# Attention weights, v, x and W_in as pairs of fp16 words, and two heads' value products on the two column halves of TensorE

## Chip, cores and metric

The kernel runs on one core of one Trainium2 chip. The metric is the device time of one execution in microseconds, as the median of several runs; lower is better. Engines are named as the profile names them: PE is TensorE (PEld its weight loads), DVE VectorE, ACT ScalarE, POOL GpSimd, SP the engine that issues the DMAs.

## What is computed

Decayed causal attention for 8 batches of 8 heads (576 positions, 64 columns a head), and on its result, laid out as 4608 tokens of 512 columns, a feed-forward layer with a softmax-weighted activation and a layer norm:

```python
def _attn_ref(q, k, v, f):
    scores = np.matmul(q, k.transpose(0, 1, 3, 2)) / np.sqrt(D)
    cum = np.cumsum(np.log(np.clip(f, 0.0001, 1.0)), axis=-1)
    scores = np.where(causal, -1e9, scores + cum[..., :, None] - cum[..., None, :])
    attn = np.exp(scores - scores.max(-1, keepdims=True))
    attn = attn / (attn.sum(-1, keepdims=True) + 1e-09)
    return np.matmul(attn, v)

def _moe_ref(x, w_in, w_out, g_ln):        # x: (4608, 512), d_ff 1024
    h = x @ w_in
    solu = h * softmax(h)
    ln = (solu - solu.mean(-1)) / np.sqrt(solu.var(-1) + 1e-06) * g_ln
    return ln @ w_out
```

The weights arrive as float64 and are unpacked to fp32 by integer operations on the chip.

## The kernel before

Products keep fp32 accuracy by splitting an operand into a high and a low word: `hi` is the value rounded to the matmul's type and `lo` the rest. Attention and the product with W_in use fp32r words (one pass of the array, operands of four bytes); the product with W_out already uses fp16 words.

**Attention** runs over 32 pairs of heads (`NPAIR` = 4 pairs in each of 8 batches), and in each pair over five tiles of queries: one of 64 rows, then four of 128. Tiles 0 to 2 are half 0 of a pair (320 queries), tiles 3 and 4 half 1 (256 queries). `load` brings q, k and v; `parts` and `split_qk` split q and k; `split_v` has POOL write v's high word (L558) and low word (L560) into `vs`, and two DMAs lay a zero-padded first block into `v0`. `scores` (L590, L591) writes score tiles to PSUM; DVE adds the mask and takes the minimum (L595), ACT takes the exponential (L598), POOL divides by the row sum (L611) into the weights P. `transposes` turns P through TensorE (L637), ACT copies the high word out of PSUM (L320) and DVE the low one (L645). `values` (L677) multiplies v and P for one head: for every block `j` of keys (three in half 0, five in half 1) one matmul with P's high word against v's high and low words side by side (128 columns of weights, so that the two results land on the two halves of PSUM's partitions), and one with P's low word against v's high word (64 columns). ACT copies one half of the partitions to `xt` (L698) and DVE adds the other (L699). The half 0 of the first four pairs, called native or early, runs in plain fp32 while the weights are still being unpacked.

**The layer** runs over 36 blocks of 128 tokens. ACT and POOL split a block of `xt` into `xh` (L710) and `xl` (L711); 24 matmuls of 512 columns (L715 to L717) give h in `hps`; DVE, ACT and POOL make the activation; 24 fp16 matmuls (L781 to L783) multiply with W_out; ACT scales the result (L813) and a DMA stores it.

**Order.** Every operation goes to a `Plan` with its engine, an assumed duration, its dependencies and a due time from tables at the top (`DUE`, `EARLY`, `AT_P`, `AT_L`, ...). The planner puts them in order for each engine; nothing is reordered on the chip, so that table numbers change the order of the whole program. Where its plan leaves PE idle in the first 140 us or after 690 us, it puts in matmuls of the identity into an unused PSUM region that nothing reads (L870, called fills below):

```python
for _ in range(int(share(t) * (y - x) / (256 * COLUMN))):
    nc.tensor.matmul(dst[:, :256], blank[:, :P], blank, start=True, stop=True)
```

Of the kernel before, what the change touches and what calls it, by code (L numbers as in the profile page):

```python
# [8 lines left out]
F32 = mybir.dt.float32  # L9
# [9 lines left out]
P = 128  # L19
# [18 lines left out]
PE, ACT, DVE, POOL, SP = range(5)  # L38
COLUMN, TRANSPOSE, SHORT = 0.4525, 109.0, 0.4215
# [3 lines left out]
W_UP, W_TOP = (1, 1, 1, 1, 3, 3, 1, 1), (1, 2, 1, 1, 1, 1, 2, 1)  # L43
# [139 lines left out]
DUE = dict(load=-21.603, split=-26.826, upper=-18.618, v=-13.364, S=((-15.632, -9.737), (-9.429, -3.796), (-5.211, -1.211), (-3.144, -0.221), (-0.983, 2.057)), T=((-5.374,), (-58.596,), (0.469, -2.051), (11.613, 15.096), (12.825, -17.362, 18.063)), V=((16.261, 10.309), (23.822, 24.94)))  # L183
EARLY = dict(load=-59.299, split=-31.676, upper=-77.592, v=4.813, S=((69.953, -64.026), (12.978, -19.27), (-10.825, -113.484), (16.361, 2.865), (6.007, 30.266)), T=((56.285,), (-26.169,), (4.567, -42.406), (18.877, 18.035), (-89.589, -1.353, 13.794)), V=((0.943, -17.263), (43.016, -5.748)))
PAIR = 23.152
C_OUT = 49.124
START = 86.674
HALF = ((21.727, 4.145), (48.927, -3.824))
W_IN = (-31.427, 49.165)
W_OUT = (167.026, 57.23)  # L190
LOAD = (91.563, -22.285)
W_SCALE = 216.178
W_DMA = (-107.022, -70.722)
LAYER = PAIR * NPAIR / 4.5
AT_P = (-22.203, 4.549, -13.13, 1.257, -1.491, 0.321, 0.679, -1.806, 5.637, 4.27, 2.052, -51.442, 0.817, -4.873, -1.256, -59.967, 1.404, 7.193, 6.528, -0.523, 0.88, -85.501, -15.204, -17.336, -23.387, -16.669, -16.683, -14.175, -4.607, -35.105, -17.856, -8.142)
AT_L = (7.435, 11.184, -2.371, 1.053, -11.997, -5.199, -4.486, -8.251, -8.484, -1.657, -2.698, 2.39, 4.153, -41.008, -6.573, -1.246, 1.043, 4.319, 5.403, -1.43, -3.146, -3.847, -8.617, -4.13, 2.145, 1.851, -3.014, -7.085, -1.035, 1.207, -5.225, -2.466, 0.361, 3.687, 6.959, 0.375)
FIRST = 96.162

STAGES = (1.419, 1.059, 4.523, 23.041, 11.635)
# [3 lines left out]
def tile_kernel(ctx: ExitStack, tc: tile.TileContext, qk, v, f, w_in, w_out, g_ln, out):  # L203
# [39 lines left out]
    v0 = [[sb(f"v0_{n}_{h}", 2 * D, dtype=F32R) for h in range(2)] for n in range(2)]  # L243
# [143 lines left out]
    dma(-90, g_sb, g_ln, 4, writes=[("g",)])  # L387

    def weights(src, n, due, t, tk, w, wk, first=(), clear=()):
# [9 lines left out]
        dma(due + W_DMA[n // NCC] if n else -98, t, src.bitcast(I32).rearrange("p (c n) -> p c n", n=512), 712 if tk[0][0] != "xt" else 940, reads=first, writes=tk)  # L401
# [23 lines left out]
    def prepare_w_in(c, due):  # L425
        w, wk = w_buffer(c % 3)
        weights(w_in[c], c, due, lambda: buf(f"wo_{c}", "raw", 4, DM, dtype=I32), [("raww", c)],
                w, wk, summed if c else ())
        copied(WI_H[c], {ACT: 1050, DVE: 690, POOL: 1130}, due, wi_h[:, c, :], w, [wk], [("wi", c)])
        op(WI_L[c], 2360 if WI_L[c] == POOL else 1170, due, lambda: (nc.gpsimd if WI_L[c] == POOL else nc.vector).tensor_tensor(  # L430
            wi_l[:, c, :], w, wi_h[:, c, :].bitcast(F32), ALU.subtract), reads=[wk, ("wi", c)], writes=[("wil", c)], port=True)
# [7 lines left out]
    def prepare_w_out(c, due):  # L439
        if c % 2:  # L440
            t, tk = xt[:, :, S:S + 512].bitcast(I32), [("xt", 1, x, hp) for x in range(2) for hp in range(NPAIR)]
# [7 lines left out]
        op(DVE, 1200, due, lambda: nc.vector.tensor_reduce(  # L449
            top[:, 2 * c:2 * c + 2], w().rearrange("p (r n) -> p r n", r=2), axis=AX.X, op=ALU.max, apply_absolute_value=True), [wk], [("top", c)])  # L450

    def scale_w_out(due):
        key = ("t", "scale")

        def across():
            nc.vector.tensor_tensor(top[:, :NFC], top[:, :NFC], g_sb, ALU.mult)
            nc.vector.tensor_reduce(top[:, NFC:], top[:, :NFC], axis=AX.X, op=ALU.max, apply_absolute_value=True)
        op(DVE, 320, due, across, [("g",), *(("top", c) for c in range(NFC // 2))], [("top",)])
        op(PE, 150, due, lambda: nc.tensor.transpose(ps_t[plan.place[key]][:1, 0, :], top[:, NFC:], ident), [("top",), ("const",)], [key], take=key, dense=False)
# [8 lines left out]
        op(PE, 150, due, lambda: nc.tensor.matmul(ps_t[plan.place[key]][:, 1, :2], ones, scales[:1, :], start=True, stop=True), [("scales",), ("ones",)], [key], dense=False)

        def factors():  # L470
            nc.vector.tensor_scalar(scales[:, 0:1], ps_t[plan.place[key]][:, 1, 0:1], 2.0 ** -24, None, ALU.mult)
            nc.vector.tensor_scalar(scales[:, 1:2], ps_t[plan.place[key]][:, 1, 1:2], 2.0 ** 13, None, ALU.mult)
            nc.vector.tensor_scalar(sg, g_sb, scales[:, 1:2], None, ALU.mult)
        op(DVE, 500, due, factors, [key, ("g",)], [("scales",), ("sg",)])
# [33 lines left out]
    def load(p, at):  # L508
# [140 lines left out]
    def values(p, half, h, at):  # L649
# [10 lines left out]
        def product(j):  # L660
# [3 lines left out]
            if j == 0 and native:  # L664
                rows, slot = row(h), 0
# [248 lines left out]
```

## Time and profile before

| | us |
|---|---|
| median of three runs | 785.98 (783.48 to 786.21) |
| the profiled execution | 783.74 |
| its span, first to last instruction | 782.0 |
| PE busy | 768.1 (98%) |
| DVE busy | 595.1 (76%) |
| ACT busy | 515.0 (66%) |
| POOL busy | 499.2 (64%) |

TensorE's granted clock was 0.999 of its full 2.4 GHz over the span. A matmul's record lasts from its start until its result has left the array, so that records of successive matmuls overlap; what a matmul takes of PE's time is read from start to start, not from the record's length.

### The profile page before, as it was taken

Reading aid. Unit: us, or ns where it says so; the run is one execution under the profiler, and the core shown is the slowest. Engines: PE = TensorE matmul, PEld = TensorE weight load, DVE = VectorE, ACT = ScalarE, POOL = GpSimd, SP = SyncE. Lnnn points to the kernel's source line nnn. Section 1 sums busy time; section 2 is a strip of 40 time slices with the busy share of each in tenths; the row PEclk is TensorE's granted clock in tenths of the full one; section 3 lists DMA queues with packets and bytes.
Section 4 is the critical chain, followed back from the end, with each engine's and each line's share of the span. In section 5 each row is a group of like instructions: output and inputs, shape, how many; then the busy total and the mean of one; then the engine's idle time right before and its main releaser. Section 6 shows DMA issues by size and latency. Waiting matters only on the chain.

```text
span 782.0 us, 15882 instructions
## 1 busy us (share of the span) xinstructions
PE 768.1 (98%) x4817; PEld 589.8 (75%) x4817; DVE 595.1 (76%) x1865; ACT 515.0 (66%) x1317; POOL 499.2 (64%) x688
## 2 busy tenths in 40 slices
PE   8999999999999999999999999999999999999998
PEld 6767678887787778777788877777777778776665
DVE  7789979997688768777679888787788688774333
ACT  5556668886677667765678777676677577664433
POOL 4556559776578577766757787777776686542230
PEclk9999999999999999999999999999999999999999
DMA  8656677766467666866658757867776656120000
GB/s 272 205 186 185 176 190 203 196 180 183 128 136 198 161 166 166 171 153 178 157 142 190 167 141 188 182 142 176 182 191 169 164 138 171 49 61 14 28 28 27
DMA packets 117012, 120.06 MB, mean 154 GB/s; under 512 B 64000, under 2 KB 78592, under 8 KB 116160
## 3 DMA queue, kind: packets, MB, share of 16 engines
q1 hardware_dynamic: 116928, 119.06, 60.3%
q8 instruction: 38, 0.62, 0.3%
q14 instruction: 46, 0.38, 0.2%
HBM read 39.11 MB, written 10.03 MB: 63 GB/s over the span
## 4 chain that ended last, share of the span: by engine, by line
PE 78%; DMA 8%; DVE 5%; SPq 3%; POOL 3%; issue 2%; ACT 1%; POOLq 0%; DVEq 0%; ACTq 0%
PE ps_o L677 12%; PE ps_t L637 10%; PE ps_o L781 7%; PE hps L715 7%; PE hps L716 7%; PE hps L717 7%; PE ps_o L782 7%; PE ps_o L783 7%; PE ps L590 5%; PE ps L591 5%; SPq L326 3%; DMA zz<-z 2%; DMA wo_raw<-in_w_in_dram 1%; DVE p L595 1%; PE ps_t L765 1%
## 5 line engine op out<-in xcount | busy, mean ns | idle before, releaser
L611 POOL TENSOR_SCALAR p<-p,ri 128x448 f32<-128x448 f32 (+4 forms) x320 | 183.1, 588 | 92.3 <-DVE ri L607 72.6
L598 ACT ACTIVATE p<-p,nm 128x192 f32<-128x192 f32 (+4 forms) x320 | 177.8, 557 | 63.7 <-DVE nm L595 54.1
L645 DVE TENSOR_TENSOR ptl_f32r<-ps_t,pth_f32r 128x384 fp32r<-128x384 f32 (+3 forms) x272 | 135.9, 518 | 26.9 <-ACT pth_f32r L320 24.5
L595 DVE CUSTOM_DVE_ANT_0 p<-ps,mask 128x192 f32<-128x192 f32 (+4 forms) x320 | 130.5, 422 | 30.7 <-PE ps L591 22.6
L320 ACT ACTIVATE pth_f32r<-ps_t 128x384 fp32r<-128x384 f32 (+3 forms) x272 | 119.3, 462 | 49.4 <-PE ps_t L637 46.7
L637 PE MATMUL ps_t<-ident,p 128*128 128x128 f32 x800 | 124.6, 274 | 1.4 <-POOL p L611 0.7
L715 PE MATMUL hps<-wi_h,xh 128*128 128x512 f32 x288 | 121.8, 423 | 0.4 <-DVE e L733 0.4
L590 PE MATMUL ps<-ks_f32r,qs_f32r 128*64 128x64 f32 (+4 forms) x360 | 120.0, 344 | 1.0 <-DVE nm L595 0.5
L637 PEld LDWEIGHTS ps_t<-ident,p 128*128 128x128 f32 x800 | 95.8, 140 | 25.3 <-DVE ptl_f32r L645 3.0
L716 PE MATMUL hps<-wi_l,xh 128*128 128x512 f32 x288 | 113.7, 395 | 0.0
L717 PE MATMUL hps<-wi_h,xl 128*128 128x512 f32 x288 | 113.7, 395 | 0.0
L781 PE MATMUL ps_o<-wo_f,zz 128*128 128x512 f16 x280 | 107.4, 384 | 1.9 <-DMA zz<-z 1.8
L782 PE MATMUL ps_o<-wo_f,zz 128*128 128x512 f16 x280 | 106.1, 379 | 1.1 <-DVE wo_f L479 1.1
L783 PE MATMUL ps_o<-wo_f,zz 128*128 128x512 f16 x280 | 106.1, 379 | 0.0
L591 PE MATMUL ps<-kz_f32r,qz 128*64 128x64 f32 (+4 forms) x360 | 103.5, 295 | 0.0
L677 PE MATMUL ps_o<-pth_f32r,vs_f32r 128*128 128x128 f32 (+1 forms) x368 | 95.1, 272 | 0.0
L590 PEld LDWEIGHTS ps<-ks_f32r,qs_f32r 128*128 128x128 f32 (+1 forms) x360 | 65.0, 181 | 16.9 <-DVE nm L595 7.8
L677 PE MATMUL ps_o<-ptl_f32r,vs_f32r 128*64 128x128 f32 (+1 forms) x368 | 71.8, 262 | 0.0
L711 POOL TENSOR_TENSOR xl<-xt,xh 128x512 fp32r<-128x512 f32 x36 | 46.0, 1278 | 40.2 <-ACT xh L710 39.7
L677 PEld LDWEIGHTS ps_o<-pth_f32r,vs_f32r 128*128 128x128 f32 x368 | 68.8, 189 | 2.5
L591 PEld LDWEIGHTS ps<-kz_f32r,qz 128*128 128x128 f32 (+1 forms) x360 | 65.2, 181 | 4.5
L726 DVE TENSOR_REDUCE st<-hps 128x1 f32<-128x1024 f32 x36 | 43.9, 1220 | 31.4 <-PE hps L717 30.9
(147 smaller groups left out, 1490.9 us busy)
## 6 DMA issues: line engine op xcount, KB each, us to landing
raw<-in_qk_dram SPq DMA_DIRECT2D x64, 288.0 KB
ks_f32r<-hi SPq DMA_DIRECT2D x128, 144.0 KB
raw<-in_v_dram SPq DMA_DIRECT2D x32, 288.0 KB
kz_f32r<-raw SPq DMA_DIRECT2D x64, 144.0 KB
out_dram<-y SPq DMA_DIRECT2D x35, 256.0 KB
qs_f32r<-hi SPq DMA_DIRECT2D x56, 144.0 KB
qs_f32r<-raw SPq DMA_DIRECT2D x56, 144.0 KB
qz<-hi SPq DMA_DIRECT2D x56, 80.0 KB
```

Source lines behind the costliest of these rows:

```text
L590: nc.tensor.matmul(dst, qs(p)[:, h, q0:q0 + nq], ks(p)[:, h, cols], start=True, stop=False)
L591: nc.tensor.matmul(dst, z[:, h, z0:z0 + nq], kz(p)[:, h, cols], start=False, stop=True)
L598: op(ACT, E_NS[i], at + 1.3, lambda: nc.scalar.activation(pr, pr, AF.Exp, bias=x, scale=-1.0, accum_out=sm[m][i][:nq, h, 0:1]), [("nm", m, ...
L611: op(POOL, N_NS[i], at + 2.8, lambda g=g, pg=pg: nc.gpsimd.tensor_scalar(pg, pg, r_[:, g:g + 1], 1.0, ALU.mult, ALU.mult), [("ri", m, i)], ...
L637: nc.tensor.transpose(tp[:, s, :], pt[i][:, k * P:(k + 1) * P], ident)
L677: nc.tensor.matmul(o[:mm, a:w], vv, mv, start=(j == 0 and x == 0), stop=(j == order[-1] and x == 0))
L715: nc.tensor.matmul(hps[:, sl], xh[:, c, :], wi_h[:, c, sl], start=(c == 0), stop=False)
L716: nc.tensor.matmul(hps[:, sl], xh[:, c, :], wi_l[:, c, sl], start=False, stop=False)
L717: nc.tensor.matmul(hps[:, sl], xl[:, c, :], wi_h[:, c, sl], start=False, stop=(c == NCC - 1))
L781: nc.tensor.matmul(o, zz[a][:, 0, j], wo(0, k), start=(k == 0), stop=False)
L782: nc.tensor.matmul(o, zz[a][:, 0, j], wo(1, k), start=False, stop=False)
L783: nc.tensor.matmul(o, zz[a][:, 1, j], wo(0, k), start=False, stop=(k == NFC - 1))
```

## The change

- P, v, x and W_in become two fp16 words. P is multiplied by 2^14 in the division by the row sum (`P_UP`). v and W_in are multiplied by a power of two found on the chip: `scale_w_in` takes the maximum of all four blocks of W_in before any is split; `scale_v` takes sums of squares of v on ACT, once for the early blocks, once for the rest of batch 0 and once for each later batch. Each of the eleven scales (`scale`, W_out's among them, which had its own code before) is a chain of DVE, PE (a transpose), DVE, PE (a product with ones), DVE. The layer undoes the scales in the operations after h (`unscale`), with one small DVE operation more per block.
- `values` takes both heads of a pair into one PSUM region. Block 0 of keys, which holds 64 rows of each head, is three full-width matmuls (L719) against a block-diagonal v. Every other block is six matmuls with 64 columns of weights (L723): high by high, low by high and high by low, each for head 0 into PSUM partitions 0 to 63 and for head 1 into 64 to 127.
- x leaves PSUM as two fp16 words (ACT, then DVE) straight into `x16`, so that the layer's split (L710, L711) is gone.
- v is loaded in a batch's four pairs together (`load_v`), its high word is made by POOL and its low word by DVE; the copies into `v0` are gone.
- The maxima for W_out's scale move from DVE (L449) to ACT (squares). All tables of due times are new.

```diff
+P_UP, SMALL = 2.0 ** 14, 2.0 ** -20
+VN, VN_EARLY = 2 * NQ, 6
...
-    wi_h, wi_l = (sb(f"wi_{x}", NCC, DFF, dtype=F32R) for x in "hl")
+    wi_h, wi_l = (sb(f"wi_{x}", NCC, DFF, dtype=F16) for x in "hl")
...
+    def scale_v(r, due):
...
+            op(ACT, 320 + 55 * (e - a), due[1] + 0.1 * hp, lambda hp=hp: nc.scalar.activation(
+                junk[:, :e - a], vraw[b % 2][:, hp, a:e], AF.Square, scale=SMALL, accum_out=tops[y][:, c + hp:c + hp + 1]),
...
     def split_v(p, at):
-        op(POOL, 650, at, lambda: nc.gpsimd.tensor_scalar(vs(p)[:, :, 0, :], rv, 1.0, 1.0, ALU.mult, ALU.mult),
-        op(POOL, 1395, at, lambda: nc.gpsimd.tensor_tensor(vs(p)[:, :, 1, :], rv, vs(p)[:, :, 0, :].bitcast(F32), ALU.subtract),
...
+        op(POOL, 860, at, lambda: nc.gpsimd.tensor_scalar(v16[m][:, 0], vraw[b % 2][:, hp], sv, 1.0, ALU.mult, ALU.mult), rk, [("v16", m)])
+        op(DVE, 740, at, lambda: nc.vector.scalar_tensor_tensor(v16[m][:, 1], vraw[b % 2][:, hp], sv, v16[m][:, 0], ALU.mult, ALU.subtract),
...
-    def values(p, half, h, at):
+    def values(p, half, at):
...
-            for x in (0, 1) if j != order[-1] else (1, 0):
...
-                    vv = (vs(p)[:, slot].rearrange("p a d -> p (a d)") if j else v0[m][h])[:, :mm]
-                    mv = ptx(p, half, x)[:, c0 + a:c0 + w]
-                nc.tensor.matmul(o[:mm, a:w], vv, mv, start=(j == 0 and x == 0), stop=(j == order[-1] and x == 0))
...
+            for n, (x, y) in enumerate(((0, 0), (1, 0), (0, 1))):
+                if j == 0:
+                    nc.tensor.matmul(o[:, :w], v16[m][:, x, :2].rearrange("p t d -> p (t d)"), ptx(p, half, y)[:, :w], start=(n == 0), stop=False)
+                    continue
+                for h in range(2):
+                    c0 = 256 * (2 * j - 1 + h)
+                    nc.tensor.matmul(o[row(h), a:w], v16[m][:, x, 2 * j + h], ptx(p, half, y)[:, c0 + a:c0 + w], start=False, stop=(end and n == 2))
...
-            nc.tensor.matmul(hps[:, sl], xh[:, c, :], wi_h[:, c, sl], start=(c == 0), stop=False)
+            x_h, x_l = (t[:, c, c0:c0 + P] for t in x16)
+            nc.tensor.matmul(hps[:, sl], x_h, wi_h[:, c, sl], start=(c == 0), stop=False)
```

**The order on PE, one pair's half 0 in the middle of the program.** Before, head 0 alone (`v0` and `vs` are v, `pth` and `ptl` P's high and low words, `ps_o` the PSUM region; the last number is the moving operand's columns):

```order
L677 MATMUL ps_o0_127<-pth_0_f32r_1547,v0_0_0_65 128x320
L677 MATMUL ps_o0_127<-ptl_0_f32r_1552,v0_0_0_65 64x320
L677 MATMUL ps_o0_127<-pth_0_f32r_1547,vs_0_f32r_809 128x128
L677 MATMUL ps_o0_127<-ptl_0_f32r_1552,vs_0_f32r_809 64x128
L677 MATMUL ps_o0_127<-ptl_0_f32r_1552,vs_0_f32r_809 64x256
L677 MATMUL ps_o0_127<-pth_0_f32r_1547,vs_0_f32r_809 128x256
```

And now, the end of the full-width products and the beginning of those on halves (`v16` is v; a weight load stands by itself for fp16):

```order
L719 LDWEIGHTS v16_0_80
L719 MATMUL ps_o0_158<-ptl_0_f16_1807,v16_0_80 128x320
L685 MATMUL ps_t0_156<-ident_61,p_0_65 128x128
L723 LDWEIGHTS v16_0_80
L723 MATMUL ps_o0_158<-pth_0_f16_1795,v16_0_80 64x128
```

The six rows of one head became three full-width matmuls and twelve on halves for both heads, the halves alternating; there are 180 of L719 in the program (84 of 320 columns, 96 of 256) and 1104 of L723 (744 of 256 columns, 360 of 128), in 98 unbroken runs.

**The order on DVE near the program's start, where W_in is unpacked.** Before, the unpacking of a block (L417, L419) is followed at once by its high word (L322):

```order
L417 SCALAR_TENSOR_TENSOR ps_o0_127<-e_109,ps_o0_127 128x512
L419 SCALAR_TENSOR_TENSOR e_109<-wo_0_raw_141,ps_o0_127 128x512
L378 TENSOR_TENSOR pth_1_cc_129<-z_110,pth_1_cc_129 64x576
L417 SCALAR_TENSOR_TENSOR ps_o1_128<-e_109,ps_o1_128 128x512
L419 SCALAR_TENSOR_TENSOR e_109<-wo_0_raw_141,ps_o1_128 128x512
L415 TENSOR_SCALAR ps_o0_127<-wo_1_raw_185 128x512
L322 TENSOR_SCALAR wi_h_103<-e_109 128x1024
```

And now the maxima of all four blocks and the chain of the scale come first (`top_wi` the maxima, `scale_wi` the scale; the first `wi_h` is at row 54 of DVE's program, where it was at row 23):

```order
L444 TENSOR_REDUCE top_wi_118<-wo_3_raw_241 128x1
L452 TENSOR_REDUCE top_wi_118<-top_wi_118 128x1
L643 ISA p_1_66,nm_0_82<-ps1_154,mask_70 128x192
L643 ISA nm_0_82 128x1
L419 SCALAR_TENSOR_TENSOR ps_o0_158<-ptl_0_w_162,ps_o0_158 128x512
L458 TENSOR_REDUCE scale_wi_122<-ps_t0_156 1x1
L460 TENSOR_SCALAR scale_wi_122<-scale_wi_122 1x1
```

W_in's words are ready later, and PE's program holds more fills: 363 before the first product with W_in (288 before), 128 between that and the last early fill (83), 12 near the end (11), in all 503 for 382.

## Rows read from the trace of the kernel before

**Rows 1.** The page: span, and busy time, share and instructions of each engine.

```profile
span 782.0 us, 15882 instructions
PE 768.1 (98%) x4817; PEld 589.8 (75%) x4817; DVE 595.1 (76%) x1865; ACT 515.0 (66%) x1317; POOL 499.2 (64%) x688
```

**Rows 2.** The page: the chain that ended last, by engine.

```profile
PE 78%; DMA 8%; DVE 5%; SPq 3%; POOL 3%; issue 2%; ACT 1%; POOLq 0%; DVEq 0%; ACTq 0%
```

**Rows 3.** Windows: stretch, its length, busy us of each engine, PEclk, DMA share.

```profile
0.00:66.00 66.00, 62.34 (x431) 44.42 (x431) 52.13 (x145) 36.65 (x93) 36.26 (x72) 1.00 0.69 217
66.00:151.00 85.00, 82.68 (x566) 66.71 (x565) 76.52 (x238) 60.35 (x156) 60.31 (x79) 1.00 0.73 189
151.00:690.00 539.00, 535.07 (x3349) 417.87 (x3349) 427.80 (x1397) 378.84 (x995) 377.36 (x504) 1.00 0.67 161
690.00:782.00 92.00, 88.06 (x478) 60.76 (x476) 38.65 (x88) 39.13 (x74) 25.27 (x34) 0.99 0.09 29
```

**Rows 4.** Windows of 20 us: one in the middle.

```profile
160.00:180.00 20.00, 19.97 (x140) 16.18 (x139) 18.89 (x64) 16.68 (x44) 14.74 (x22) 1.00 0.73 195
```

**Rows 5.** Timeline of PE, products with W_in: start us, us, instruction.

```profile
402.55 0.40 PE L715 MATMUL hps<-wi_h,xh 128*128 128x512 f32 x1
...
403.71 0.39 PE L717 MATMUL hps<-wi_h,xl 128*128 128x512 f32 x1
```

**Rows 6.** Timeline of PE, products with W_out.

```profile
407.27 0.38 PE L782 MATMUL ps_o<-wo_f,zz 128*128 128x512 f16 x1
...
408.13 0.38 PE L783 MATMUL ps_o<-wo_f,zz 128*128 128x512 f16 x1
```

**Rows 7.** Timeline of PE, value products.

```profile
414.13 0.28 PE L677 MATMUL ps_o<-pth_f32r,vs_f32r 128*128 128x256 f32 x1
414.25 0.28 PE L677 MATMUL ps_o<-ptl_f32r,vs_f32r 128*64 128x256 f32 x1
...
414.60 0.22 PE L677 MATMUL ps_o<-pth_f32r,vs_f32r 128*128 128x128 f32 x1
```

**Rows 8.** Groups by shape, PE and its weight loads: busy us, mean ns, idle before.

```profile
L677 PEld LDWEIGHTS ps_o<-pth_f32r,vs_f32r 128*128 128x128 f32 x368 | 68.8, 189 | 2.5
L677 PEld LDWEIGHTS ps_o<-ptl_f32r,vs_f32r 128*64 128x64 f32 x368 | 41.0, 135 | 0.8
L782 PEld LDWEIGHTS <-zz 128*128 128x128 f16 x280 | 27.7, 99 | 14.7
L716 PE MATMUL hps<-wi_l,xh 128*128 128x512 f32 x288 | 113.7, 395 | 0.0
```

**Rows 9.** Timeline of PE, a run of fills and what follows it.

```profile
36.30 2.69 PE L870 MATMUL hps<-ident 128*128 128x256 bf16 x23
38.82 0.71 PE L637 MATMUL ps_t<-ident,p 128*128 128x128 f32 x5
```

**Rows 10.** Windows of the fills alone (L870): length, PE, PEld, PEclk, DMA share.

```profile
0.00:66.00 66.00, 36.38 (x288) 27.89 (x288) 1.00 0.69 217
66.00:151.00 85.00, 12.30 (x85) 7.76 (x83) 1.00 0.73 189
151.00:690.00 539.00, 0.00 (x0) 0.00 (x0) 1.00 0.67 161
```

**Rows 11.** Groups by shape on DVE and POOL that the change removes, or prices.

```profile
L699 DVE TENSOR_TENSOR xt<-ps_o,xt 64x320 f32<-64x320 f32 x56 | 27.2, 485 | 6.0 <-ACT xt L698 5.1
L699 DVE TENSOR_TENSOR xt<-ps_o,xt 64x256 f32<-64x256 f32 x64 | 26.8, 420 | 9.0 <-ACT xt L698 7.8
L530 DVE TENSOR_TENSOR raw<-raw,hi 128x576 fp32r<-128x576 f32 x32 | 26.4, 826 | 5.9 <-POOL hi L527 5.7
L734 DVE TENSOR_SCALAR st<-st 128x1 f32<-128x1 f32 x36 | 5.5, 153 | 1.5
L711 POOL TENSOR_TENSOR xl<-xt,xh 128x512 fp32r<-128x512 f32 x36 | 46.0, 1278 | 40.2 <-ACT xh L710 39.7 <-PE ps L591 0.5
L560 POOL TENSOR_TENSOR vs_f32r<-raw,vs_f32r 128x576 fp32r<-128x576 f32 x32 | 46.8, 1463 | 2.3
```

More of the change, by code (lines that the diff above doesn't have):

```diff
@@ L185 @@
[L185 to L193, printed above, removed]
+DUE = dict(load=4.152, split=-9.177, upper=-24.66, v=-10.796, S=((-16.648, -10.814), (-9.29, -2.745), (-3.828, -8.056), (-5.79, 0.256), (-0.823, 3.345)), T=((-4.854,), (-6.326,), (0.491, -3.167), (11.082, 13.131), (12.289, -35.219, 17.674)), V=((15.397, 228.659), (24.445, 27.85)))
@@ new lines @@
+EARLY = dict(load=-67.132, split=-12.664, upper=-76.728, v=-31.832, S=((113.142, -154.277), (57.237, -18.28), (28.269, -190.437), (-31.944, 23.119), (12.778, 46.97)), T=((61.422,), (-55.149,), (-14.527, -36.338), (-6.382, -12.696), (-171.163, -95.685, -35.587)), V=((5.496, -10.8), (54.516, -55.939)))
+PAIR = 23.242
+C_OUT = 78.693
+START = 86.699
+HALF = ((9.767, 8.464), (53.286, -13.942))
+W_IN = (-35.782, 57.012)
+W_OUT = (129.947, 50.69)
+LOAD = (138.489, -29.189)
+WI_SCALE = (-18.507, -120.396)
@@ L426, in prepare_w_in @@
         w, wk = w_buffer(c % 3)
[L427 to L431, printed above, removed]
+        t, tk = (lambda: buf(f"wo_{c}", "raw", 4, DM, dtype=I32)), [("raww", c)]
@@ new lines, in prepare_w_in @@
+        weights(w_in[c], c, due, t, tk, w, wk, summed if c else ())
+        sw = scales["wi"][:, 1:2]
+        copied(WI_H[c], {ACT: 1050, DVE: 690, POOL: 1130}, due, wi_h[:, c, :], w, [wk, ("scale", "wi")], [("wi", c)], scale=sw)
+        if WI_L[c] == POOL:
+            copied(ACT, {ACT: 1050}, due, w, w, [("wi", c), ("scale", "wi")], [wk], scale=sw)
+            op(POOL, 2360, due, lambda: nc.gpsimd.tensor_tensor(wi_l[:, c, :], w, wi_h[:, c, :], ALU.subtract), reads=[wk, ("wi", c)], writes=[("wil", c)])
+        else:
+            op(DVE, 1170, due, lambda: nc.vector.scalar_tensor_tensor(wi_l[:, c, :], w, sw, wi_h[:, c, :], ALU.mult, ALU.subtract),
+               reads=[wk, ("wi", c), ("scale", "wi")], writes=[("wil", c)], port=True)
@@ new lines, in scale_w_in @@
+    def scale_w_in(due):
+        for c in range(NCC):
+            dma(W_IN[0] + W_IN[1] * c + W_DMA[0] if c else -98, lambda c=c: buf(f"wo_{c}", "raw", 4, DM, dtype=I32),
+                w_in[c].bitcast(I32).rearrange("p (c n) -> p c n", n=512), 712, reads=summed if c else (), writes=[("raww", c)])
+            op(DVE, 1220, due[0] + c, lambda c=c: nc.vector.tensor_reduce(
+                tops["wi"][:, c:c + 1], buf(f"wo_{c}", "raw", 4, DM, dtype=I32).bitcast(F32).rearrange("p c (n t) -> p c n t", t=2)[:, :, :, 1],
+                axis=AX.XY, op=ALU.max, apply_absolute_value=True), [("raww", c)], [("top", "wi", c)])
+        scale("wi", "wi", NCC, due[1])
@@ L433, in wo32, with unscaled @@
+    def unscaled(n):
+        r = [0 if t < HALF_S else t // S + 1 for t in (n * P, n * P + 64)]
+        if r[0] == r[1]:
+            return unscale[r[0]], [("un", r[0])]
+        key = (r[0], r[1])
+        for y in range(2):
+            op(POOL, 150, -60, lambda y=y: nc.gpsimd.tensor_copy(unscale[key][row(y)], unscale[r[y]][row(y)]), [("un", r[y])], [("un", key, y)])
+        return unscale[key], [("un", key, 0), ("un", key, 1)]
     def wo32(k):
@@ L452, in scale_w_out @@
     def scale_w_out(due):
[L453 to L459, printed above, removed]
@@ L468, in scale_w_out @@
[L468 to L473, printed above, removed]
@@ L822, in half_of @@
                 transposes(p, i, g, at + due["T"][i][g])
-        for h in range(2):
-            values(p, half, h, at + due["V"][half][h])
+        values(p, half, at + due["V"][half][0])
     done = 0
@@ L847, in tile_kernel @@
     layers(HALF_S)
+    load_v(0, HALF[1][0] + VDUE[1][0])
+    scale_v(1, [HALF[1][0] + x for x in VDUE[1]])
     for p in range(NPAIR):
```

208 lines of the change are left out of this document (118 added, 90 removed).

## Prediction

> **What bounds the kernel now.** I read the engines' shares first: PE is busy for 768.1 of 782.0 us, no other engine above 76% [rows 1]. A busy PE may still be waiting inside long records, so the chain of waits comes next: 78% of the path to the last instruction runs through PE, DMA has 8%, DVE 5% [rows 2]. Then the windows, by stage. From 151 to 690 us PE is busy 535.1 of 539.0 us with no fills [rows 3, 10]; there time is matmul work, and what a change takes off PE is worth its full length. Before 66 us it is otherwise: of 62.3 us of PE, 36.4 us are fills [rows 3, 10], so PE waits there for weights to be unpacked, and PE work saved there is worth nothing. From 66 to 151 us both mix. The granted clock is at its upper level throughout, 2.4 GHz.
>
> **Prices on PE, from start to start.** Five steps between 402.55 and 403.71 give 232 ns for an fp32r matmul of 512 columns [rows 5]; four steps between 407.27 and 408.13 give 215 ns for an fp16 one [rows 6], 0.42 ns a column. Four value matmuls of 256 columns between 414.13 and 414.60 take 117.5 ns each [rows 7]. Fills: 23 in 2.52 us, 110 ns each [rows 9].
>
> **Products with W_in.** 36 blocks of 24 matmuls, 864, go from 232 to 215 ns: 864 x 17 ns = **14.7 us saved**. Their weights load faster too (fp16 99 ns against 189 [rows 8]), but both are hidden by the stream, so nothing is added for it.
>
> **Value products, before.** The 28 later pairs' half 0 stream 320 + 256 + 128 = 704 columns, the 32 halves 1 stream 4 x 256 + 128 = 1152, each four times (two heads, two matmuls): 78,848 + 147,456 = 226,304 columns, at 117.5 ns per 256 **103.9 us**.
>
> **Value products, after.** The 180 full-width matmuls have 84 x 320 + 96 x 256 = 51,456 columns: 21.6 us at 0.42 ns. The 1104 on halves form 552 pairs. No row of before shows two matmuls side by side in the array, so their price is bounded: if the halves overlap fully, a pair costs one stream, 107.5 ns at 256 columns and 54 ns at 128; if not at all, twice that. Weight loads can limit the short ones: 64 columns less make a load 189 - 135 = 54 ns shorter [rows 8], so 64 columns occupy the load path for 54 ns and two loads 108 ns, as long as a stream of 256 columns and twice one of 128. I take overlap with serial loads: 372 x 107.5 + 180 x 108 ns = 40.0 + 19.4 = 59.4 us, with the full-width ones 81.0 us, **22.9 us saved**. Ends: 71.3 us with free loads, 121.0 us without overlap (80.0 + 19.4 + 21.6). I take it nearer to the lower end because alternate 64- and 128-column matmuls already follow each other at their stream's pace [rows 7].
>
> The Trainium skill (TensorE: Matmul & The Clock Gate, Part 3, Measured speedup) gives 2.38 times for three column tiles of 32. Scaled to two tiles, as an estimate from that page, 0.63 of the time without overlap; the value products would be 84 us and the sum 3 us worse. No run here shows it yet.
>
> **Fills and small products.** The order holds 121 more fills. They are issued whether or not PE would have waited: 121 x 110 ns = **13.3 us added**, 75 of them (8 us) ahead of the first product with W_in. That is the price of finding W_in's scale first. It could be as little as 7 us if 6.0 us of them fall where PE idled before (66.0 - 62.3 and 85.0 - 82.7 [rows 3]). Ten scale chains more are 20 small PE instructions, priced like fills: **2.2 us**. The native value products may overlap too, but lie under fills: nothing.
>
> **The other engines.** DVE: the 120 additions into xt (27.2 + 26.8 us) become 60 operations of the same widths, -27.0 us; v's low word, 32 x 640 columns at the 826 ns per 576 of a like split, is 32 x 0.92 = +29.4 us; 36 + 10 x 8 small ones at 153 ns, +17.7 us [rows 11]; maxima of W_in for those of W_out, even. In all some +20 us, 615. POOL loses the splits of x and of v's low word, 46.0 + 46.8 us [rows 11], and keeps v's high word: near 407. ACT trades the cast of x and half of 120 copies for 44 squares; with a third of its time free [rows 1] I put that at nothing. SP issues 64 copies into v0 less; DMA is 8% of the chain and keeps its load. What hides the DVE work is PE: in the middle DVE has 427.8 of 539 us [rows 3] and would have some 446 of 509, 88%. In one window it had 18.89 of 20 us while PE was busy 19.97 [rows 4]; so I count no new wait, but this is the cover that is thinnest.
>
> **Sum.** -14.7 - 22.9 + 13.3 + 2.2 = -22.1 us. Span 782.0 - 22.1 = 759.9; the execution profiled took 783.74, so **762 us**. That execution stands 2.2 us below the median of 785.98, within the runs' spread of 783.48 to 786.21. About 0.5% is what a measurement of this kernel can tell from no change.
>
> **Rivals.**
> *The halves do not overlap.* Then the change does not do what it says, value products take 121.0 us, 40 us more than I count: 802 us, slower. It decides where a pair costs 1.38 times one half: 82 instead of 59.4 us of pairs eats the whole gain. For it: no row shows overlap. Against it: weight loads do run beside matmuls of other weights, PEld is busy 589.8 us inside PE's 768.1 [rows 1]. Chance 0.09.
> *The array empties at every change of tile width.* There are 98 runs of half-width matmuls, 196 changes; an emptied array costs what a record outlasts its stream, 395 - 232 = 163 ns [rows 8, 5]: +32 us, 794 us. Against it: 128- and 64-column tiles alternate in the value products of before at 117.5 ns, their stream's own length [rows 7]. The Trainium skill (TensorEngine Tiling (Array Packing), Key Properties) says that a change of tiling mode drains the TensorE. By that rule these rows should show the cost, and they do not. Chance 0.05.
> *DVE sets the pace.* If it cannot get past its 79% of the middle stretch, because its waits for ACT and PE come with the work, 446 us need 562 us instead of 509: 815 us. At 84% the gain is just gone, 784 us, and this is its likeliest form. For it: DVE's work grows while everything around it shrinks. Against it: the 94% of [rows 4], and POOL, ahead of DVE in the splits, gets some 90 us lighter. Chance 0.12, of it 0.05 within 0.5%, 0.03 faster and 0.04 slower.
>
> **How the numbers follow.** The forecast has 0.74: its own range is 762 - 9.7 (free loads) - 6.0 (fills in old idle time) = 746 to 762 + 14 (PE's idle 782.0 - 768.1 doubled [rows 1]) = 776. With the third rival: faster 0.77, same 0.05, slower 0.04 + 0.09 + 0.05 = 0.18. The range of 745 to 790 takes in the forecast's own bounds and the third rival's likely form, and leaves out the first two and its worst end.
>
> **What would show it.** In the profile after: successive L723 of the two halves overlapping, a pair of 256 columns each 108 ns or so, not 215; products with W_in 215 ns apart; the first of them near 75 us instead of 66; no group of waits of PE on DVE worth over 14 us; DVE near 615, POOL near 407 us busy. The prediction is wrong if pairs are 150 ns or more apart, if every run of L723 begins or ends with a gap of 0.1 us or more, or if PE idles in the middle stretch.

## Result and profile after: half the forecast gain

The changed kernel takes **774.55 us** (median of 4 executions, 772.28 to 777.73) against 786.10 us of the kernel before on the same chip: ratio **0.986**, interval 0.982 to 0.991. In a later set of runs (e11) it took 771.50 us, ratio 0.984 (0.982 to 0.987). The forecast was 762 us: the direction holds and the time lies in the range, but of some 24 us of gain 12 to 14 came. The profiled execution has a span of 774.2 us and took 776.02 us.

The page after: span, engines, and the chain by engine, against [rows 1, 2].

```profile
span 774.2 us, 16702 instructions
PE 759.1 (98%) x5276; PEld 483.3 (62%) x5276; DVE 605.8 (78%) x1946; ACT 507.0 (65%) x1316; POOL 426.2 (55%) x640
...
PE 74%; DVE 10%; POOL 2%; ACT 1%; DMA 1%; issue 1%; SPq 0%; DVEq 0%; POOLq 0%; ACTq 0%
```

PE is still the bound: busy 98% and three quarters of the chain. DVE has 605.8 us (forecast 615), POOL 426.2 (forecast 407). In the chain DMA gave its share up and DVE doubled its own.

The windows after, in the columns of [rows 3] (PE, PEld, DVE, ACT, POOL, PEclk, DMA share, GB/s):

```profile
0.00:66.00 66.00, 59.42 (x426) 44.90 (x427) 45.38 (x135) 37.74 (x95) 29.98 (x67) 0.92 0.60 188
66.00:151.00 85.00, 82.04 (x632) 57.69 (x630) 74.43 (x236) 65.28 (x168) 45.88 (x68) 1.00 0.71 204
151.00:690.00 539.00, 536.85 (x3763) 337.46 (x3763) 453.13 (x1512) 374.11 (x1003) 335.22 (x485) 1.00 0.66 159
690.00:774.00 84.00, 80.75 (x461) 43.29 (x459) 32.88 (x66) 29.82 (x52) 15.16 (x22) 1.00 0.10 32
```

In the middle PE idles only 2.2 us of 539.0, less than the 3.9 of before [rows 3]. So no wait that shows took the gain. What PE is busy with must be longer than counted, and the timeline shows where. PE, two value products on halves (L723) with what stands ahead of and behind them; columns as in [rows 5], xN counts matmuls that the view puts in one line:

```profile
463.63 0.27 PE L685 MATMUL ps_t<-ident,p 128*128 128x128 f32 x1
463.83 0.30 PE L723 MATMUL ps_o<-pth_f,v 128*64 128x128 f16 x4
463.97 0.22 PE L723 MATMUL ps_o<-ptl_f,v 128*64 128x128 f16 x2
464.02 0.39 PE L723 MATMUL ps_o<-pth_f,v 128*64 128x256 f16 x4
464.24 0.28 PE L723 MATMUL ps_o<-ptl_f,v 128*64 128x256 f16 x2
464.45 0.39 PE L757 MATMUL hps<-wi_h,x_h 128*128 128x512 f16 x1
...
479.64 0.27 PE L719 MATMUL ps_o<-ptl_f,v 128*128 128x256 f16 x1
479.84 0.41 PE L723 MATMUL ps_o<-pth_f,v 128*64 128x256 f16 x4
```

Three things are to be read here.
- **The halves overlap.** From 464.02 to 464.24 four matmuls of 256 columns take 0.22 us, 110 ns a pair, the time of one stream.
- **Short pairs cost less than I counted.** From 463.83 to 464.02 three pairs of 128 columns take 0.19 us: the first 80 ns, the others 56 and 55. Over the program the median behind the first pair of a run is 56 ns at 128 columns and 109 at 256, the time of one stream; the first pair takes some 25 ns more (80 and 134). I had 108 for the short ones, for weight loads one after the other.
- **A change between 128 and 64 columns costs 0.1 us, each way.** L719 at 479.64 streams 256 columns, 107.5 ns; the next start is 200 ns later. The last pair, at 464.24, needs 107.5 ns; the next product follows after 210.

Taking from the interval across either end of a run of L723 the stream of the instruction ahead (columns at 0.42 ns), the 172 changes between 150 and 690 us carry 18.2 us, 0.10 to 0.11 us each. At 0.10 us the 196 of the program are 19.6 us, and this is the price that the runs below go by. It is not all of it: the step behind a change is longer too. With that step, and against the same places in e1 below, where no change is left, the 196 are 26.0 us, 0.13 each.

The weight loads show where the time goes:

```profile
463.50 0.14 PEld L685 LDWEIGHTS ps_t<-ident,p 128*128 128x128 f32 x1
463.83 0.42 PEld L723 LDWEIGHTS <-v 128*64 128x64 f16 x12 [0.19 <-issue]
464.45 0.10 PEld L757 LDWEIGHTS <-x_h 128*128 128x128 f16 x1 [0.20 <-issue]
```

Between 150 and 690 us a load's record begins 108 ns (median) ahead of its matmul's, under the stream before. At all 172 changes it begins within 5 ns of its matmul. The price of a change, against e1, follows the length of that load: 100 to 118 ns on entry (loads of 106), 106 on leaving for an fp16 product (96), 150 for a transpose (138), 193 for an fp32r score product (186). That a change costs one load that nothing hides is read from these sizes; no run tests it.

The products with W_in came out as forecast: from the first L757 to the L827 behind its triple, 409.88 to 410.53, are three steps of 217 ns.

```profile
409.88 0.38 PE L757 MATMUL hps<-wi_h,x_h 128*128 128x512 f16 x1
...
410.53 0.38 PE L827 MATMUL ps_o<-wo_f,zz 128*128 128x512 f16 x1
```

The groups of the new DVE work: busy us, mean ns, idle before. v's low word took 31.1 us (forecast 29.4).

```profile
L611 DVE SCALAR_TENSOR_TENSOR v<-vraw,scale,v 128x640 f16<-128x640 f32 x32 | 31.1, 976 | 1.5 <-POOL v L610 1.4
L741 DVE SCALAR_TENSOR_TENSOR x_l<-ps_o,x_h 128x256 f16<-128x256 f32 (+1 forms) x60 | 26.9, 448 | 5.4 <-ACT x_h L740 5.3
```

### The profile page after: what moved, and what is told of

It is laid out like the page before. It is cut to its first block, busy times and chain, and to the rows that moved or that the text cites. A ratio compares the mean times of both kernels' runs of the same rounds, so it can differ in the third digit from the quotient of the medians.

```text
span 774.2 us, 16702 instructions
## 1 busy us (share of the span) xinstructions
PE 759.1 (98%) x5276; PEld 483.3 (62%) x5276; DVE 605.8 (78%) x1946; ACT 507.0 (65%) x1316; POOL 426.2 (55%) x640
## 4 chain that ended last, share of the span: by engine, by line
PE 74%; DVE 10%; POOL 2%; ACT 1%; DMA 1%; issue 1%; SPq 0%; DVEq 0%; POOLq 0%; ACTq 0%
PE ps_t L685 10%; PE hps L757 7%; PE ps_o L827 7%; PE hps L759 7%; PE hps L758 7%; PE ps_o L829 7%; PE ps_o L828 7%; PE ps_o L723 7%; PE ps L638 6%; PE ps L639 5%; PE ps_o L719 2%; DVE p L643 2%; DVE ptl_f L693 1%; DVE v L611 1%; DVE st L770 1%; PE ps_t L811 1%
## 5 line engine op out<-in xcount | busy, mean ns | idle before, releaser
L659 POOL TENSOR_SCALAR p<-p,ri 128x320 f32<-128x320 f32 (+4 forms) x320 | 187.7, 600 | 126.4 <-DVE ri L655 78.8
L326 ACT ACTIVATE pth_f<-ps_t 128x384 f16<-128x384 f32 (+5 forms) x284 | 124.6, 456 | 72.8 <-PE ps_t L685 65.5
L693 DVE TENSOR_TENSOR ptl_f<-ps_t,pth_f 128x384 f16<-128x384 f32 (+3 forms) x272 | 135.6, 517 | 17.1 <-ACT pth_f L326 15.7
L638 PE MATMUL ps<-ks_f32r,qs_f32r 128*128 128x192 f32 (+4 forms) x360 | 133.8, 381 | 1.7 <-DVE nm L643 1.0
L757 PE MATMUL hps<-wi_h,x_h 128*128 128x512 f16 x288 | 110.3, 383 | 0.2 <-DVE e L779 0.2
L758 PE MATMUL hps<-wi_l,x_h 128*128 128x512 f16 x288 | 109.2, 379 | 0.0
L759 PE MATMUL hps<-wi_h,x_l 128*128 128x512 f16 x288 | 109.2, 379 | 0.0
L827 PE MATMUL ps_o<-wo_f,zz 128*128 128x512 f16 x280 | 107.3, 383 | 0.1
L639 PE MATMUL ps<-kz_f32r,qz 128*128 128x192 f32 (+4 forms) x360 | 103.2, 294 | 0.0
L639 PEld LDWEIGHTS ps<-kz_f32r,qz 128*128 128x128 f32 (+1 forms) x360 | 65.5, 182 | 3.5
L646 ACT ACTIVATION_READ_ACCUMULATOR p<-p,nm 128x1 f32 (+1 forms) x320 | 60.5, 189 | 0.0
L723 PE MATMUL ps_o<-pth_f,v 128*64 128x256 f16 (+1 forms) x736 | 59.1, 262 | 0.0
```

Of the source, the lines that this page charges most:

```text
L638: nc.tensor.matmul(dst, qs(p)[:, h, q0:q0 + nq], ks(p)[:, h, cols], start=True, stop=False)
L639: nc.tensor.matmul(dst, z[:, h, z0:z0 + nq], kz(p)[:, h, cols], start=False, stop=True)
L646: op(ACT, E_NS[i], at + 1.3, lambda: nc.scalar.activation(pr, pr, AF.Exp, bias=x, scale=-1.0, accum_out=sm[m][i][:nq, h, 0:1]), [("nm", m, ...
L659: op(POOL, N_NS[i], at + 2.8, lambda g=g, pg=pg: nc.gpsimd.tensor_scalar(pg, pg, r_[:, g:g + 1], 1.0 if native else P_UP, ALU.mult, ALU.mu ...
L757: nc.tensor.matmul(hps[:, sl], x_h, wi_h[:, c, sl], start=(c == 0), stop=False)
L758: nc.tensor.matmul(hps[:, sl], x_h, wi_l[:, c, sl], start=False, stop=False)
```

## Experiments

**e1, one head's products at full width.** Every block after the first becomes three full-width matmuls; head 1's products are left out. The order is that of the changed kernel, with no change of width left.

```diff
-                for h in range(2):
-                    c0 = 256 * (2 * j - 1 + h)
-                    nc.tensor.matmul(o[row(h), a:w], v16[m][:, x, 2 * j + h], ptx(p, half, y)[:, c0 + a:c0 + w], start=False, stop=(end and n == 2))
+                c0 = 256 * (2 * j - 1)
+                nc.tensor.matmul(o[:, a:w], v16[m][:, x, 2 * j:2 * j + 2].rearrange("p t d -> p (t d)"), ptx(p, half, y)[:, c0 + a:c0 + w], start=False, stop=(end and n == 2))
```

> The changed kernel, but every block after the first is three full-width matmuls (both heads' v as 128 columns of weights) that stream head 0's P alone; head 1's products of these blocks are left out, and cross terms stand in their place. The streams are as long as those of perfectly overlapping halves, and the order is the same, but no change of tile width is left. Theory A (each of the 196 changes between full-width and half-width weights costs PE 0.1 us, read from the start-to-start times of the changed kernel): 774.5 - 196 x 0.1 = 755 us, ratio to before 0.961. Theory B (VectorE sets the pace in the middle, the gaps are where PE waits anyway): 771 to 775 us, ratio 0.982 to 0.986.

764.41 us, ratio 0.973 (0.971 to 0.975): between the two. The gaps are gone. From 472.69 to 472.80 a 256-column L719 is followed in 110 ns, and in the middle the same sum over the ends falls from 18.2 to 0.5 us.

```profile
472.46 0.39 PE L719 MATMUL ps_o<-pth_f,v 128*128 128x256 f16 x2
472.69 0.27 PE L719 MATMUL ps_o<-ptl_f,v 128*128 128x256 f16 x1
472.80 0.38 PE L722 MATMUL ps_o<-pth_f,v 128*128 128x256 f16 x2
```

But of 19.6 us only 10 arrive (9 by the ratios, against e11). From the first product with W_in to PE's last instruction the traces have 693.2 us in e11, 3.2 of them idle, and 683.1 in e1, 9.8 of them idle. So PE's own time fell by 16.7 us and 6.6 came back as waits. The steps had 26.0; where the rest went, no run shows. PE's waits (us, times, longest) now lead with POOL and DVE, each 1.0 us or less in the changed kernel; in the middle the idle time that the view ascribes to a releaser is 7.2 us, where the changed kernel on the later chip (e11) has 1.4.

```profile
PE ps_t L685 <- POOL p L659: 3.8, 7, 0.8
...
PE ps L638 <- DVE nm L643: 3.3, 6, 0.9
```

**e6, e1 with less work on DVE.** Of v's low word DVE makes one column of 640; the rest of it is left out, and head 1 as in e1.

```diff
-        op(DVE, 740, at, lambda: nc.vector.scalar_tensor_tensor(v16[m][:, 1], vraw[b % 2][:, hp], sv, v16[m][:, 0], ALU.mult, ALU.subtract),
+        op(DVE, 740, at, lambda: nc.vector.scalar_tensor_tensor(v16[m][:, 1, :1], vraw[b % 2][:, hp, :1], sv, v16[m][:, 0, :1], ALU.mult, ALU.subtract),
```

> The run with full-width matmuls of one head only (764.4 us), with v's low word on DVE cut to one column of 640 (32 times some 0.9 us of DVE less, 29 us); leaves out head 1's products and all but one column of v's low word. Theory A, what that run did not give of the 19.6 us (9 us) is the pace of DVE: 756 to 759 us, and the waits for DVE's negated maxima fall. Rival B, it is the order or POOL that holds it: 763 to 765 us.

757.83 us, ratio 0.964 (0.962 to 0.966): the time of theory A. Its second sign failed: the waits for DVE's maxima stay (3.0 us), and so do those for POOL. Some of the 6.6 us between the two medians is a start without a fall of the clock (see e3); against e1's one execution at a mean clock of 1.00, 762.41 us, it is 4.6 us. DVE's work thus sets part of the pace once PE is shorter; through which wait, the profile does not show.

**e7, the same relief on the changed kernel** (the edit of e6 alone).

> The changed kernel with v's low word on DVE cut to one column of 640 (29 us of DVE less); leaves out the rest of that word. Theory A, in the changed kernel PE with its changes of width is the bound and DVE has slack: 772 to 775 us. Rival B, DVE's added work is itself a reason why the gain was smaller than forecast: 766 us or less.

771.80 us, ratio 0.981 (0.978 to 0.984). The two medians of the changed kernel are 774.55 and 771.50: against the first e7 is 2.8 us less, against the second nothing. It is just under theory A's range and far from rival B's. With its changes of width PE is slow enough for DVE.

**e4, both heads in the first half of the columns** (the second overwrites the first in places; the sums are left out).

```diff
-                    nc.tensor.matmul(o[row(h), a:w], v16[m][:, x, 2 * j + h], ptx(p, half, y)[:, c0 + a:c0 + w], start=False, stop=(end and n == 2))
+                    nc.tensor.matmul(o[row(0), a:w], v16[m][:, x, 2 * j + h], ptx(p, half, y)[:, c0 + a:c0 + w], start=(n == 0 and h == 0), stop=(n == 2 and h == 1))
```

> The changed kernel, but both heads' half-width products go to PSUM partitions 0 to 63, each block overwriting the one before it; the sums over blocks and head 1's place are left out. Tells what the 0.1 us belongs to. If to the width of the fp16 weights: entry and exit of a run still show 0.1 us. If to the use of the second column half: they vanish. Either way the halves cannot overlap: 372 x 107.5 + 180 x 54 ns = 50 us more of PE, 820 us or so, if overlap is what keeps a pair at 110 ns.

819.02 us, one execution: without overlap the change would have cost time. The timeline separates the two effects. Four matmuls of 256 columns now take 0.43 us (498.21 to 498.64), 108 ns each; the gaps at both ends stay, 0.23 us behind an L719 of 320 columns (134 ns) and 0.31 us behind two of 256 (215 ns).

```profile
497.62 0.30 PE L719 MATMUL ps_o<-ptl_f,v 128*128 128x320 f16 x1
497.85 0.41 PE L723 MATMUL ps_o<-pth_f,v 128*64 128x128 f16 x4
498.09 0.28 PE L723 MATMUL ps_o<-ptl_f,v 128*64 128x128 f16 x2
498.21 0.60 PE L723 MATMUL ps_o<-pth_f,v 128*64 128x256 f16 x4
498.64 0.38 PE L723 MATMUL ps_o<-ptl_f,v 128*64 128x256 f16 x2
498.95 0.55 PE L685 MATMUL ps_t<-ident,p 128*128 128x128 f32 x3
```

So the gap belongs to these matmuls of 64 columns, not to the second half and not to two matmuls side by side.

**e2, runs merged.** Value products of one region that stand apart are moved back to the next of that region where nothing between needs them: 60 runs instead of 98. The core of the edit:

```diff
+                while n < len(order) and of.get(order[n][1].seq) != k and order[n][1].seq not in users:
+                    n += 1
+                if n < len(order) and of.get(order[n][1].seq) == k and n > i + 1:
+                    order.insert(n - 1, order.pop(i))
```

> The changed kernel, complete, with one edit of the order: value products of one region that stand apart are moved back to just before the next of the same region, where nothing between needs them. Runs of half-width matmuls go from 98 to 60. Theory A: 38 runs less, two changes each, 0.1 us a change: -7.6 us, 767 us, ratio 0.976. Theory B: no change within 1 us, or slower, since products that were ready are held back: ratio 0.985 to 0.990.

783.43 us, ratio 0.999 (0.997 to 1.000): 9 us slower than the changed kernel, which neither theory foresaw. The gaps did shrink, from 18.2 to 10.7 us in the middle, but PE idles 11.7 us there, some 8 of them for DVE. The waits of the whole run:

```profile
PE ps L638 <- DVE nm L643: 6.6, 14, 1.3
...
PE ps_t L685 <- DVE ptl_f L693: 2.1, 4, 0.9
```

A product moved back holds P's words longer, and DVE writes the next ones later. I argue this from the waits; no run separates it.

**e5 and e12, runs merged where little stands between.** One or two PE instructions go ahead of the run before them, where the order has them ready by then: 75 runs, 46 changes fewer.

```diff
+            if n < len(order) and good and 0 < len(others) <= NEAR and max(order[x][1].ready for x in others) <= order[i][0]:
+                moved = [order[x] for x in run]
+                order[others[-1] + 1:others[-1] + 1] = moved
```

> One or two instructions of PE that stand between two runs of half-width value matmuls go ahead of the first run, where the order has them ready by then: 75 runs instead of 98, everything else as in the changed kernel. Theory A, each change of width costs 0.1 us of PE's path and little else is disturbed: 46 changes fewer, 4.6 us, so 770 us (ratio to the kernel before 0.980). Rival B, moves on PE cost as much in waits as they save, as in the run with 60 runs: 774 us or more (0.986 or more).

770.92 us, ratio 0.983 (0.980 to 0.985). As the changed kernel scatters by its start, both ran again side by side:

> The changed kernel itself, beside the next run on the same chip: 774.5 us (0.986).

> The kernel with 75 runs of half-width matmuls instead of 98, beside the changed kernel on the same chip. Theory A (46 changes of width at 0.1 us): 4 us below the changed kernel, 770 us (0.981). Rival B, the 3.6 us between the two so far are the scatter of the start: within 1.5 us of it.

e11: 771.50 us (0.984, 0.982 to 0.987); e12: 772.41 us (0.983, 0.982 to 0.985). Rival B of e12 holds: a gain cannot be told from the scatter. Among executions at a mean clock of 1.00, e5 has 770.0 to 770.9 us and the control 771.0 to 772.3: 1 us or so, not 4.6. The gaps in the middle are 4.1 us less in e5 than in the control, while PE idled 4.9 us there instead of the control's 2.0. No version here clearly beats the changed kernel.

**e13 and e14, changes added and nothing moved.** The last runs all moved or left out other work. These put one small matmul ahead of each half block of products with W_in, 72 in all, into columns that the product overwrites: 64 columns of weights (e13) or 128 (e14).

```diff
+            if c == 0:
+                nc.tensor.matmul(hps[:64, 512 * a:512 * a + 64], x_h[:, :64], wi_h[:, 0, :64], start=True, stop=True)
```

> The changed kernel with one matmul more ahead of each half block of products with W_in, 72 in all: fp16, 64 columns of weights, 64 columns streamed, into columns of PSUM that the product behind it overwrites. 68 of them stand between full-width instructions and add two changes of width each; nothing is moved. Theory A, a change of width takes 0.1 us of PE's path whoever makes it: 68 x 0.2 + 72 x 0.027 = 15.5 us more, 786 to 789 us (1.002 to 1.005). Rival B, the 0.1 us seen at the value products belongs to their operands or their place, or is hidden: 773 to 777 us (0.985 to 0.990).

> The same 72 matmuls with 128 columns of weights instead of 64, so that no change of width is added. Theory A: 72 x 0.03 to 0.06 us, 773 to 776 us (0.985 to 0.989). Rival B, one more small instruction costs as much as the narrow one, whatever its width: within 3 us of the run before this one.

e13: 790.20 us, ratio 1.005 (1.003 to 1.007), 1 us over theory A's range. e14: 778.67 us, ratio 0.991 (0.990 to 0.993), 3 us over theory A's range and far from rival B's; all its executions have a mean clock of 0.996 (see the start, below). Their difference is the price of 136 changes alone: 11.5 us, 85 ns each. The timelines, e13 first:

```profile
402.48 0.36 PE L639 MATMUL ps<-kz_f32r,qz 128*128 128x448 f32 x1
402.77 0.22 PE L758 MATMUL hps<-wi_h,x_h 128*64 128x64 f16 x1
402.92 0.39 PE L759 MATMUL hps<-wi_h,x_h 128*128 128x512 f16 x1
```

```profile
401.88 0.22 PE L639 MATMUL ps<-kz_f32r,qz 128*64 128x64 f32 x1
401.95 0.21 PE L758 MATMUL hps<-wi_h,x_h 128*128 128x64 f16 x1
401.99 0.38 PE L759 MATMUL hps<-wi_h,x_h 128*128 128x512 f16 x1
```

A stream of 64 columns is 27 ns. The narrow matmul holds PE for 150 ns and begins 290 ns after one that streams 448 fp32r columns (203 ns); the wide one holds it for 40. The row ahead of it in e14 is an fp32r matmul with 64 columns of weights, and the full-width start follows it after 70 ns, where a stream of 29 and a change of 100 would make 130.

It is not the width by itself. In six places of the changed kernel an fp32r matmul with 64 columns of weights (L639) stands right ahead of a value product on halves, 64 columns as well. In the same six places of e1 the product is full width. The changed kernel first:

```profile
460.83 0.22 PE L639 MATMUL ps<-kz_f32r,qz 128*64 128x64 f32 x1
460.99 0.41 PE L723 MATMUL ps_o<-pth_f,v 128*64 128x256 f16 x4
```

```profile
453.21 0.22 PE L639 MATMUL ps<-kz_f32r,qz 128*64 128x64 f32 x1
453.28 0.40 PE L722 MATMUL ps_o<-pth_f,v 128*128 128x256 f16 x2
```

From start to start it is 153 ns in all six places of the changed kernel and 63 in all six of e1. An fp32r matmul of 64 columns thus counts as full width; the price lies between fp16 matmuls of 64 columns and everything else.

**e10, W_in alone.** The kernel before with only W_in's and x's words as fp16, unscaled.

```diff
-    wi_h, wi_l = (sb(f"wi_{x}", NCC, DFF, dtype=F32R) for x in "hl")
+    wi_h, wi_l = (sb(f"wi_{x}", NCC, DFF, dtype=F16) for x in "hl")
...
-    xh, xl = (sb(f"x{x}", NCC, P, dtype=F32R) for x in "hl")
+    xh, xl = (sb(f"x{x}", NCC, P, dtype=F16) for x in "hl")
```

> The kernel before with the two words of W_in and of x as fp16 (unscaled) and nothing else: the 864 products with W_in go from 232 to 215 ns. Theory A, as forecast for that term: 14.7 us less, 771 us (0.981). Rival B, in the order of before the saved time turns into waits for DVE or POOL, and under half of it arrives: 779 us or more (0.991 or more).

778.79 us, ratio 0.992 (0.990 to 0.994). Rival B: the products are 215 ns apart as forecast, but only 6.4 of 14.7 us arrive. In the middle PE idles 9.2 us instead of 3.9; the two waits that grew most over the whole run, from 0.4 and 0.7 us before:

```profile
PE ps_t L637 <- DVE ptl_f32r L645: 2.5, 6, 1.4
PE ps_t L637 <- POOL p L611: 2.4, 5, 0.8
```

**e3, e8 and e9, the start.** e3 puts 24 more fills ahead of the first score of the second early pair; e8 leaves every fourth early fill out; e9 sets W_in's scale to a constant and leaves its search out.

```diff
+                if not wake and o.take and o.take[:2] == ("s", 1):
+                    wake = True
+                    for _ in range(24):
+                        nc.tensor.matmul(hps[:, :256], blank[:, :P], blank, start=True, stop=True)
```

```diff
+                        fills += 1
+                        if fills % 4 or t > 200.0e3:
-                        nc.tensor.matmul(dst[:, :256], blank[:, :P], blank, start=True, stop=True)
+                            nc.tensor.matmul(dst[:, :256], blank[:, :P], blank, start=True, stop=True)
```

```diff
+            nc.vector.memset(scales["wi"][:, c:c + 1], 2.0 ** (34 * c - 17))
...
-            op(DVE, 1220, due[0] + c, lambda c=c: nc.vector.tensor_reduce(
+            op(DVE, 1220, due[0] + c, lambda: None, [("raww", c)], [("top", "wi", c)])
```

> The changed kernel, complete, with 24 fills more ahead of the first score product of the second early pair, where PE waited 2.1 us for a DMA at 36 us and ran at the lower clock for some 10 us after it. Theory C (the clock's fall in the start is on the path to the end): granted clock 1.00 from 36 to 48 us, first product with W_in some 4 to 5 us earlier than 78 us, 769 to 771 us, ratio 0.979 to 0.981. Rival D (the start is set by the unpacking of W_in on VectorE and its transfers): the clock stays up, but the first product with W_in stays at 77 to 79 us and the time within 1 us of 774.5, ratio 0.986.

> The changed kernel without every fourth of the early fills, 122 of 491 (13.4 us of PE). Theory A, the fills are what holds the first product with W_in back: it starts at about 68 to 70 us instead of 76 to 78, and the time is 766 us (0.975). Rival B, the fills only cover what PE waits for anyway (W_in's scale and words): the first product stays at 75 to 78 us and the time is 773 to 776 us.

> The changed kernel with W_in's scale set to the constant that the search finds: four maxima on DVE, the two small operations on PE and the scale chain of W_in left out; order, fills and all else as before. Theory A, the search for W_in's scale is what makes the first product with W_in start some 8 to 12 us later: it starts at 72 us or earlier and the time is 768 us or less (0.977 or less). Rival B, the early attention itself, in its new order, holds that product (its last operand is the low word of the fourth early pair's values): the start moves by under 2 us and the time is 772 to 775 us.

e3: 773.73 us (ratio 0.986, 0.984 to 0.988), its first product with W_in at 75.6 us. e8: 775.01 us (0.987, 0.985 to 0.990), that product at 76.6 us. e9: 773.64 us (0.985, 0.983 to 0.987), that product at 73.95 us. In the control (e11) the product starts at 73.3 us with fills and search. So the search is not what holds it, as rival B of e9 says.

On the fills the runs are less clear. In e3 the clock stayed up as theory C says, but the product came 2.7 us earlier, not 4 to 5, and not at rival D's 77 to 79 either; against the control it is 2.3 us later, about the 2.6 us of the 24 fills. e8 has the time and the product of rival B, but its granted clock fell to 0.65 from 36 to 48 us, behind 3.1 us of waiting for a DMA, so it does not tell what its fills cost at the upper clock. The 78.3 us of the first profile have another cause. Windows from 36 to 48 us of the changed kernel, and of e11:

```profile
36.00:48.00 12.00, 11.52 (x45) 7.71 (x46) 3.81 (x18) 5.48 (x19) 2.66 (x4) 0.57 0.58 215
```

```profile
36.00:48.00 12.00, 11.04 (x85) 8.69 (x84) 8.04 (x39) 9.75 (x33) 7.20 (x11) 1.00 0.52 196
```

PE's timeline just ahead of that, of the changed kernel and of e11; in brackets the idle time before the instruction and what ended it:

```profile
36.32 1.19 PE L636 MATMUL ps<-kz_k,qs_q 65*128 65x320 f32 x3 [2.08 <-DMA kz_k<-p]
```

```profile
35.29 1.05 PE L636 MATMUL ps<-kz_k,qs_q 65*128 65x320 f32 x3 [0.26 <-DMA kz_k<-p]
```

Where PE had waited 2.08 us for a DMA, the granted clock went to its lower level of 1.2 GHz (0.50 from 40 to 44 us); where it waited 0.26 us it stayed at 2.4 GHz. Of the nine executions of the changed kernel the three with a mean clock of 0.995 or less took 776.0 to 777.7 us, the six others 771.0 to 773.1.

## Why the prediction was half right

**Right.** The halves overlap and the products with W_in go at 215 ns; PE stays the bound; it idles less, not more; DVE is 9 us under and POOL 19 us over its forecast, neither of them deciding. The first rival (no overlap) is what e4 looks like, 17 us dearer than its 802. The third (DVE sets the pace) did not happen in the changed kernel, as e7 shows. That the time lies in the forecast's own 746 to 776 us is luck: the upper end was made for PE's idle time doubled, and PE idled less.

**The step that failed** is the rival that I gave a chance of 0.05, "the array empties at every change of tile width". The sum has nothing for it. A cost at every change is there, and the sign of being wrong that I had named for it, a gap of 0.1 us at the ends of every run of L723, is there: 196 changes, 19.6 us by the intervals across, 26.0 us with the steps behind. The 163 ns each that I took from [rows 8, 5] were no measurement, since the profile models where a matmul's record ends. I set it aside on [rows 7], where 128- and 64-column matmuls alternate at the pace of their stream. Those rows are fp32r, and the new ones are fp16: e13 and e14 show that only the latter pay, and the six places beside L639 that an fp32r matmul of 64 columns counts as full width. A row was taken as evidence for an operation of another data type. The rule I had named beside it, of the Trainium skill (TensorEngine Tiling (Array Packing), Key Properties), is that a change of tiling mode drains the TensorE. The traces agree with it for fp16, with 0.09 us a change in run time (e13 against e14) and 0.13 in the steps. Why fp32r matmuls of 64 columns count as full width, no run here shows.

**The term that was mis-sized the other way** is the pairs: 372 at 109 ns and 180 at 56 ns, 50.6 instead of 59.4 us, with what the first pair of a run takes more counted to the change. Weight loads of two halves do not queue behind each other as I assumed: a pair's two loads have records of some 110 ns that begin 3 to 4 ns apart. The estimate from the Trainium skill (TensorE: Matmul & The Clock Gate, Part 3, Measured speedup) put a pair at 0.63 of two single ones; 109 of 215 ns is 0.51.

**The sum, mended.** 759.9 + 26.0 - 8.8 = 777.1 us. The control's span is 769.7. Of the 7.4 us between them, 1.9 are PE's shorter idle time in the middle (3.9 to 2.0), and 1.7 the start at 73.3 instead of 75 us; 3.8 us stay open, so some other term is mis-sized, and the runs do not say which. The first profile adds 4.5 us by its fall of the clock (774.2 against 769.7), which I had not considered because the trace of before holds its upper level.

**The fills** are a term that no run settles. I priced 121 of them at 13.3 us as work that delays. In e3 the 24 added ones did about that, 2.3 us of the start. In e8, without 122 of them, PE waits instead, its clock is lower (0.65 from 36 to 48 us), and the time stays.

**"What a change takes off PE is worth its full length" is too strong.** e10 got 6.4 of 14.7 us and e1 10 of 19.6: in both, waits for DVE and POOL took at least part of the rest. In the changed kernel the gaps kept PE slow enough that it idled no more than before. With the gaps gone, part of my sum would still not have arrived.

## What to carry to other kernels

Two fp16 matmuls of 64 columns do run side by side in the two column halves, at the price of one. Entering and leaving them cost 0.1 to 0.2 us each here, so runs must be long enough to earn 0.2 to 0.3 us, and this belongs in the costs of whatever plans the order. Clear a rival only by a row of the same data type and shape. Where a second engine has 80% of a stretch, as DVE has in e10 and e1, half or less of what PE saved arrived; count on no more until a run says otherwise. Moving work in a tuned order for a few gaps gained nothing clear (e5, e12) or lost 9 us (e2).

## What was not expected of the hardware

- Entering or leaving fp16 matmuls of 64 columns costs PE 0.10 to 0.19 us in the steps, about the length of the next weight load. Between fp32r matmuls of 128 and 64 columns nothing shows, and one of 64 columns counts as full width.
- Pairs of 128 streamed columns on opposite halves follow each other at 56 ns, though each matmul has a weight load of its own.
- One wait of PE for a DMA goes with the clock of what follows: behind 0.3 to 0.6 us (e5, e6, e9, e11) the upper level stayed; behind 1.1 to 3.5 us (e1, e2, e4, e8, e12, e13, e14 and the first profile) the clock was at the lower level for 7 to 10 us, which is worth some 5 us from one execution to the next.
